# An attention-and-two-MLP kernel: a new hand-written order of the first part, and PSUM pools cut differently

## The chip, the cores and the metric

One core of a Trainium2 chip. The metric is the device time of one execution in microseconds, from the first to the last instruction and what lies around them. TensorE is called PE, VectorE DVE, ScalarE ACT, GpSimd POOL and SyncE SP, as in the profile.

## What is computed

Attention over 4 batches, 8 heads, 576 positions of 64 features: a downsampled attention (mean of four positions, repeated four times) plus a local one within a band of 3 positions. Its output is the input `x` (2304 x 512) of two MLPs, all in float32:

```python
out_d = sm_attn(q_d, k_d, v_d)                      # on means over 4 positions
out_up = np.repeat(out_d, factor, axis=2)
scores = np.where(np.abs(pos[:, None] - pos[None, :]) < factor, scale * q @ k.T, -1e9)
attn_out = out_up + softmax(scores) @ v
h = x @ w_in                                        # 512 -> 2048
x2 = (h * np.cos(h)) @ w_out                        # 2048 -> 512
out = ((x2 @ w_a) * (x2 @ w_b)) @ w_out2            # 512 -> 1536 -> 512
```

## The kernel before

The weights arrive as float64 and are turned into float32 on the chip. Matrix products in float32 are made of three passes with a rounded high part and a low remainder of each operand (`mm3`, L575 to L579, printed as L576, L577 and L578 in the profile), so every operand has to be split: a copy that rounds (the high part, "hi" or "gh") and a subtraction (the low part, "lo" or "gl").

There are two parts. The first runs attention (8 units of 288 rows) and the first MLP (7 blocks of 288 or 432 rows and 16 slices of 128 features, cut to 112 steps), and prepares the weights of the second MLP. The second part is the second MLP, in which each product is made of seven smaller ones (P1 to P7) with sums before and after; its order comes from loops and is not part of the list below.

The first part's order is written out by hand: `ORDER` is a list of 2791 keys, and a loop (L933) takes them one by one and calls the function behind each. `InOrder` (L192) then ties each engine's instructions to the order in which they were written; between the engines only data and free buffers make one wait for the other. A key with `@a`, `@d` or `@p` also says which engine runs it: ACT, DVE or POOL. SP's loads and stores have keys of their own (L, F and S) and go through one queue in the order of the list.

The keys that matter here:

- `w<t>.0` to `w<t>.4`: weight tile t from float64 to float32 and split. 0 and 1 on ACT (L275, L278), 2 on DVE (L280, all operands in SBUF), 3 the rounded copy (L292 on ACT, L294 on DVE), 4 the remainder (L569, DVE or POOL).
- `h<g>.<c>`: the three matmuls of input chunk c of step g into a bank of PSUM ("h", two of them). `c<g>.0` to `c<g>.6`: h times cosine of h. 0 on ACT, 1 on DVE (L629, reads PSUM), 2 on ACT, 3 square (L634 ACT or L636 DVE), 4 on DVE (L638, reads PSUM and frees the h bank), 5 rounded copy gh (L292 or L294), 6 remainder gl (L644, DVE or POOL). `b<g>.<m>`: the matmuls into the four banks "acc".
- attention of unit u: `sm` and `vs` sums over four positions (a reduction on DVE, L360 and L351, or three additions on POOL, L362 to L364, L353 and L355), `lp`, `dp` scores, `lm` and `dx` maxima (L390, L395, L413), `lu`, `da` subtractions, `le`, `de` exponentials, `ln`, `dn` sums, `lz`, `dz` divisions, `lt`, `dt` transposes, `lc`, `dc` copies back, `at` products, `up`, `cb` sums of the two, `xh`, `xl` the split of the result into the tile `xbig` (L294 or L292, and L550).
- `p<n>.*`: weights of the second MLP, converted, combined and stored to DRAM; `x<i>.*`: loads, sums and splits of the second MLP's first input; `F`: its first weight loads.

PSUM has eight banks: four "acc", two "h" and one tile "att" of two banks for attention, all from one pool `ps`. In the second part `banks_of` (L999) hands them out as two sets of four, set 0 being the two halves of "att" and the two "h". `split_g` (L968) also borrows banks of the set that is not in use for a copy of gh (L988), four at a time.

Of the kernel before, what the change touches and what calls it, by code (L numbers as in the profile page):

```python
# [48 lines left out]
L0s2 vs0.2@p h1.1 le0.1 ln0.1 lz0.1@d w2.3@a w2.4@d w4.3@a w4.4@p L0w7 w7.1@a w7.0@a w3.4@p lt0.1 lc0.10@d lc0.11@a L0w5 w5.0@a w5.1@a w7.2@d w5.2@d  # L49
at0.1 up0.1@a cb0.2 xh0.2@d xl0.2@p h0.2 cb0.3 h1.2 L0w6 w6.0@a xh0.3@d xl0.3@p h0.3 w6.1@a w6.2@d w5.3@a w5.4@p Lc8 w8.1@a w8.0@a Lq1.0 sm1.0@d  # L50
w6.3@a Lq1.1 sm1.1@d w8.2@d Lq1.2 h1.3 w6.4@p c0.0@a c1.0@a c0.1@d c0.2@a Lc10 lp1.0 c1.1@d c1.2@a lm1.0 lu1.0@p w8.3@d c0.3@a Lc12 lu1.1@p Lc11
c0.4@d c0.5@d c0.6@p dp1.0 dx1.0 c1.3@a c1.4@d w8.4@p da1.00@d c1.5@d c1.6@p Lq2.2 h2.0 h2.1 h2.2 h2.3 da1.01@d sm1.2@p w12.0@a w10.0@a Lq1.3 sm1.3@d
le1.0 ln1.0 Lk2.2 b0.3 Lk2.3 Lc14 b0.1 h3.0 c2.0@a lz1.0@p h3.1 c2.1@d de1.0 lp1.1 lm1.1 Lc9 b1.1 w11.0@a lu1.3@p b1.3 dn1.0 dz1.1@p b0.2 w11.1@a h3.2
h3.3 w11.2@d c2.2@a Lk2.0 Lq2.1 dp1.1 dx1.1 Lc18 c3.0@a c2.3@a w10.1@a c2.4@d w7.3@a w14.0@a lu1.2@p c3.1@d c3.2@a Lw2.0 b1.2 da1.10@d c2.5@d b0.0 L0V
da1.11@d b1.0 w11.3@d w10.2@d dz1.0@p h4.0 h4.1 h4.2 w9.1@a h4.3 c4.0@a c2.6@p lt1.0 lc1.01@d w7.4@p w9.0@a w9.2@d b2.1 c3.3@a b2.2 b2.3 b2.0 lc1.00@a
c3.4@d Lc13 Lc15 w11.4@p w9.3@d w9.4@p dt1.0 dc1.0@d h5.0 h5.1 w10.3@d w10.4@p Lk2.1 le1.1 ln1.1 lz1.1@p w12.1@a c4.1@d c3.5@d h5.2 h5.3 w14.1@a de1.1
at1.0 up1.0@a cb1.0 Lq2.0 cb1.1 c3.6@p w12.2@d lt1.1 b3.2 w13.1@a c4.2@a xh1.0@d lc1.10@a dn1.1 w14.2@d c4.3@a c4.4@d vs2.0@p c5.0@a b3.1 c5.1@d Lc17
w15.1@a dz1.3@p c4.5@d Lc16 xh1.1@a c5.2@a w12.3@d dz1.2@p xl1.1@d lc1.11@a c4.6@p b3.3 c5.3@a b3.0 c5.4@d w15.0@a h6.0 h6.1 h6.2 w12.4@p h6.3 dt1.1
c6.0@a sm2.0@d c5.5@d h7.0 dc1.1@a h7.1 h7.2 c6.1@d w15.2@d w14.3@a w13.0@a w13.2@d w16.0@a at1.1 up1.1@a cb1.2 w16.1@a b4.2 cb1.3 w16.2@d c6.2@a
xl1.0@p Lc27 w14.4@p Lw2.1 vs2.1@p Lc19 h7.3 c7.0@a c7.1@d b4.1 c6.3@a c6.4@d xh1.2@a xl1.2@p xh1.3@a xl1.3@p c7.2@a sm2.1@d b4.0 Lc21 w13.3@a c5.6@p  # L60
w19.1@a Lc25 lp2.0 b4.3 c7.3@a lm2.0 c7.4@d h8.0 h8.1 h8.2 w17.1@a h8.3 c8.0@a c8.1@d dp2.0 Lw2.2 w13.4@p c6.5@a c6.6@d Lq2.3 h9.0 vs2.2@p h9.1 h9.2
dx2.0 Lc20 w21.0@a b5.2 lu2.0@p da2.01@d h9.3 b5.1 Lq3.0 Lc28 da2.00@d w17.0@a b5.0 b6.0 sm2.2@d lu2.1@p lp2.1 c8.2@a w15.3@a c7.5@a w15.4@p c7.6@p
c8.3@a c8.4@d c9.0@a c9.1@d b5.3 h10.0 h10.1 w19.0@a w19.2@d lm2.1 le2.0 b6.2 ln2.0 Lw2.3 vs2.3@p c9.2@a h10.2 h10.3 lu2.2@p c10.0@a c10.1@d c9.3@a
c9.4@d Lv2 b6.1 b7.1 e7.1@a lu2.3@p b7.0 e7.0@d c8.5@a c8.6@p c10.2@a c10.3@a Lq3.2 Lc26 sm2.3@d c10.4@d b7.2 b6.3 b7.3 e7.3@d c10.5@d Lw2.4 h12.0
# [1159 lines left out]
```

## Time and profile before

| | us |
|---|---|
| median of 3 runs | 953.74 (951.58 to 954.83) |
| profiled execution | 953.3 |
| its span, first to last instruction | 951.4 |
| PE busy | 898.7 |
| DVE busy | 729.0 |
| ACT busy | 574.3 |
| POOL busy | 551.9 |

The profile is of one execution. An engine counts as busy from the start of an instruction to its end, whatever happens in between, so a duration is to be held against the shortest of its kind. The granted clock is TensorE's, as a share of its full speed.

### The profile page before, as it was taken

How to read it: one execution, taken by the hardware profiler on the slowest of the kernel's cores; microseconds unless marked ns; L12 is line 12 of the kernel's file. 1: busy time of each engine (PE TensorE's matmuls, PEld its weight loads, DVE VectorE, ACT ScalarE, POOL GpSimd, SP SyncE). 2: the span in 40 equal slices, each digit the busy share in tenths (PEclk: the TensorE clock that was granted, in tenths of full speed). 3: DMA queues.
4: the chain of work that ended last, by engine and by line, in shares of the span. 5: the costliest groups of instructions: out<-in, count | busy, mean ns of one | idle time of the engine just before them, and what ended most of it. 6: DMA issues, size and time to landing. Idle time of an engine off the chain costs nothing.

```text
span 951.4 us, 18829 instructions
## 1 busy us (share of the span) xinstructions
PE 898.7 (94%) x6828; PEld 862.7 (91%) x6828; DVE 729.0 (77%) x1329; ACT 574.3 (60%) x1237; POOL 551.9 (58%) x689
## 2 busy tenths in 40 slices
PE   3688979999999999999989999999999999999998
PEld 2587878999999999899989899999999999999997
DVE  6999998888698986864688488869667678767754
ACT  5797867565486785843675355548544466544473
POOL 5697879365266773721473266746467754677540
PEclk9789999999999999999999999999999999999999
DMA  9475622245465676400798145594753266832631
GB/s 294 166 264 192 189 83 67 64 129 158 122 207 172 183 203 187 139 21 7 241 308 251 60 151 165 173 401 168 243 211 111 89 245 238 317 109 71 220 148 51
DMA packets 97582, 162.13 MB, mean 170 GB/s; under 512 B 6736, under 2 KB 63568, under 8 KB 97488
## 3 DMA queue, kind: packets, MB, share of 16 engines
q1 hardware_dynamic: 97488, 160.92, 51.0%
q8 instruction: 54, 0.88, 0.4%
q14 instruction: 40, 0.33, 0.1%
HBM read 127.66 MB, written 33.23 MB: 169 GB/s over the span
## 4 chain that ended last, share of the span: by engine, by line
PE 73%; DVE 15%; issue 5%; POOL 3%; ACT 3%; DMA 1%; SPq 0%; DVEq 0%; POOLq 0%; ACTq 0%
PE z L576 14%; PE z L578 13%; PE z L577 13%; PE h L576 5%; PE h L577 5%; PE h L578 5%; PE acc L576 5%; PE acc L577 4%; PE acc L578 4%; DVE raw L280 2%; DVE gs L638 1%; DVE gs L629 1%; PE att L510 1%; PE att L383 1%; PE att L503 1%
## 5 line engine op out<-in xcount | busy, mean ns | idle before, releaser
L966 POOL TENSOR_TENSOR sb<-w,sb 128x256 fp32r<-128x256 f32 x154 | 124.7, 821 | 112.8 <-ACT sb L964 104.8
L576 PE MATMUL h<-xbig,w 128*128 128x288 f32 (+1 forms) x448 | 147.3, 329 | 14.8 <-DVE gs L638 12.3
L576 PE MATMUL acc<-gh,w 128*128 128x288 f32 (+1 forms) x448 | 144.1, 322 | 0.8 <-DVE yp L613 0.8
L577 PE MATMUL h<-xbig,w 128*128 128x288 f32 (+1 forms) x448 | 142.0, 317 | 1.5 <-DVE xbig L550 1.2
L578 PE MATMUL h<-xbig,w 128*128 128x288 f32 (+1 forms) x448 | 141.9, 317 | 0.0
L577 PE MATMUL acc<-gl,w 128*128 128x288 f32 (+1 forms) x448 | 140.8, 314 | 1.0 <-POOL gl L644 0.6
L578 PE MATMUL acc<-gh,w 128*128 128x288 f32 (+1 forms) x448 | 140.2, 313 | 0.0
L964 ACT ACTIVATE sb<-w 128x256 fp32r<-128x256 f32 x252 | 97.6, 414 | 64.2 <-PE z L578 54.9
L644 POOL TENSOR_TENSOR gl<-gs,gh 128x288 fp32r<-128x288 f32 (+1 forms) x66 | 64.9, 986 | 91.0 <-DVE gh L294 59.3
L576 PEld LDWEIGHTS h<-xbig,w 128*128 128x128 f32 x448 | 86.0, 192 | 21.6 <-DVE gs L638 15.8
L576 PE MATMUL z<-xbig,sb 128*128 128x384 f32 x288 | 97.6, 341 | 2.7 <-DVE g L1027 1.3
L578 PE MATMUL z<-xbig,sb 128*128 128x384 f32 x288 | 97.0, 338 | 0.2 <-POOL sb L966 0.2
L577 PE MATMUL z<-xbig,sb 128*128 128x384 f32 x288 | 97.1, 337 | 0.0
L627 ACT ACTIVATE gs<-h 128x288 int32<-128x288 f32 (+1 forms) x112 | 49.3, 440 | 68.3 <-PE h L578 63.8
L577 PEld LDWEIGHTS h<-xbig,w 128*128 128x128 f32 x448 | 86.2, 192 | 2.9 <-DVE xbig L550 1.4
L576 PEld LDWEIGHTS acc<-gh,w 128*128 128x128 f32 x448 | 84.7, 189 | 4.4 <-issue 2.2
L577 PEld LDWEIGHTS acc<-gl,w 128*128 128x128 f32 x448 | 84.7, 189 | 2.8 <-POOL gl L644 1.1
L578 PEld LDWEIGHTS h<-xbig,w 128*128 128x128 f32 x448 | 86.1, 192 | 1.0
L578 PEld LDWEIGHTS acc<-gh,w 128*128 128x128 f32 x448 | 84.5, 189 | 1.0
L631 ACT ACTIVATE gs<-gs 128x288 f32<-128x288 f32 (+1 forms) x112 | 53.4, 477 | 46.8 <-DVE gs L629 46.3
L966 DVE TENSOR_TENSOR sb<-w,sb 128x256 fp32r<-128x256 f32 x98 | 60.6, 621 | 21.1 <-ACT sb L964 20.8
L629 DVE SCALAR_TENSOR_TENSOR gs<-gs,h 128x288 f32<-128x288 int32 (+1 forms) x112 | 54.6, 488 | 27.4 <-ACT gs L627 26.3
(158 smaller groups left out, 2510.2 us busy)
## 6 DMA issues: line engine op xcount, KB each, us to landing
w<-wd SPq DMA_DIRECT2D x63, 512.0 KB
w<-wd_a SPq DMA_DIRECT2D x18, 512.0 KB
w<-wd_b SPq DMA_DIRECT2D x18, 512.0 KB
raw<-in_w_in_dram SPq DMA_DIRECT2D x16, 512.0 KB
raw<-in_w_out_dram SPq DMA_DIRECT2D x16, 512.0 KB
w<-wd_a SPq DMA_DIRECT2D x18, 384.0 KB
w<-wd_b SPq DMA_DIRECT2D x18, 384.0 KB
praw<-in_w_a_dram SPq DMA_DIRECT2D x12, 512.0 KB
```

The costliest lines, as they stand in the source:

```text
L280: dve.scalar_tensor_tensor(out=lw if out is None else out, in0=hh, scalar=3, in1=lw, op0=ALU.logical_shift_left, op1=ALU.bitwise_or)
L383: pe.matmul(p[i][o, W * w:W * w + W], qt[u, 2 * pr + i][r, off:off + W], kt[u // 2, 2 * pr + i][r, BASE[half] + off:BASE[half] + off + W], ...
L503: pe.matmul(p[i][64 * a:64 * a + 64, NB:NB + QD], vdt[b, hp][:, a, c], pd[u, hp][:, 2 * a + c], start=(c == 0), stop=(c == 1),)
L576: i = pe.matmul(ps_out, lh, rh, start=start, stop=False, skip_group_check=more)
L577: pe.matmul(ps_out, lh, rl, start=False, stop=False, skip_group_check=more)
L578: pe.matmul(ps_out, ll, rh, start=False, stop=stop, skip_group_check=more)
L627: act.activation(out=gs[g].bitcast(I32), in_=hps[g], func=AF.Copy, scale=1.0 / (2.0 * math.pi))
L629: dve.scalar_tensor_tensor(out=gs[g], in0=gs[g].bitcast(I32), scalar=-2.0 * math.pi, in1=hps[g], op0=ALU.mult, op1=ALU.add)
L631: act.activation(out=gs[g], in_=gs[g], func=AF.Sin, scale=0.5)
L644: eng.tensor_tensor(out=gl[g], in0=gs.pop(g), in1=gh[g].bitcast(F32), op=ALU.subtract)
L964: act.activation(out=t[:, 0], in_=blk, func=AF.Copy)
L966: (dve if nst[0] % (C["SD"] if G else C["SD0"]) == 0 else pool).tensor_tensor(out=t[:, 1], in0=blk, in1=t[:, 0].bitcast(F32), op=ALU.subtract)
```

## The change

The list `ORDER` is replaced. It has the same 2791 keys in another order, and some keys name another engine. The new list was made by a planner that lets an operation of VectorE which works in SBUF alone and an operation of POOL never run at the same time. Of the engines named in the whole list, above all these differ: `w.4` on DVE 2 before and 12 after (on POOL 30 and 20), `c.5` on DVE 65 and 46 (on ACT 47 and 66), `c.3` on DVE 41 and 36, `c.6` on DVE 46 and 51, `vs` on DVE 10 and 12, `xl` on DVE 9 and 12, `lz` on DVE 2 and 4.

Beside it, attention's tile "att" moves to a pool `pa` of its own, which closes with attention's SBUF pool. The second part opens a pool `pz` in its place with two tiles of one bank each, and the borrowed banks for L988 are taken one at a time, in turn. The diff, with nearly all lines of the two lists left out:

```diff
 ORDER = """
-L0k0 L0q1 L0q0 sm0.0@d L0k1 L0w1 w1.1@a w1.0@a lp0.0 sm0.1@d lm0.0 dp0.0 dx0.0 da0.01@d da0.00@a L0k2 de0.0 L0s1 L0q2 w1.2@d vs0.1@d lu0.0@p lu0.1@p
-le0.0 sm0.2@p dn0.0 dz0.1@a dz0.0@a dt0.0 L0q3 ln0.0 L0w0 w0.1@a w0.0@a L0k3 lz0.0@p sm0.3@d dp0.1 dx0.1 lt0.0 w1.3@a w1.4@p dc0.0@a da0.11@a da0.10@d
-L0s0 vs0.0@p L0w3 lc0.01@d w0.2@d w0.3@d lc0.00@a de0.1 dn0.1 dz0.3@p L0v w3.0@a at0.0 w3.1@a w3.2@d dz0.2@a up0.0@a cb0.0 cb0.1 L0w4 w0.4@p w3.3@a
-xh0.1@a xl0.1@p xh0.0@d lp0.1 dt0.1 L0w2 w2.1@a w2.0@a xl0.0@d h0.0 h0.1 h1.0 lm0.1 lu0.2@d w2.2@d w4.0@a lu0.3@p w4.1@a w4.2@d L0s3 vs0.3@p dc0.1@a
...
-b109.2 b110.2 b111.2 S111.1 e111.2@a S111.2
+L0k0 L0q0 sm0.0@d L0k1 L0q1 lp0.0 lm0.0 lu0.0@d L0w1 w1.0@a w1.1@a sm0.1@p dp0.0 dx0.0 da0.01@d w1.2@d L0q2 L0k2 sm0.2@d lu0.1@p le0.0 ln0.0 L0s0
+vs0.0@p da0.00@a L0w0 de0.0 lz0.0@d lt0.0 w0.0@a w1.3@a dn0.0 w1.4@d w0.1@a dz0.0@a dz0.1@a dt0.0 w0.2@d w0.3@d L0s1 L0q3 L0k3 sm0.3@d dp0.1 dx0.1
+da0.10@d vs0.1@p L0w2 lc0.00@a L0v w0.4@d lc0.01@a dc0.0@a at0.0 w2.1@a L0s2 w2.0@a w2.2@d w2.3@d w2.4@p da0.11@a de0.1 dn0.1 up0.0@a cb0.0 xh0.0@a
+cb0.1 xh0.1@d dz0.3@a Lq1.0 sm1.0@d lp0.1 lm0.1 lu0.3@d lu0.2@d dz0.2@a xl0.0@p L0w4 h0.0 w4.0@a w4.1@a w4.2@d Lq1.1 sm1.1@d le0.1 w4.3@a L0w3 w3.0@a
...
+b111.0 e111.0@d S111.0
...
@@ -225,6 +225,7 @@
     dram = ctx.enter_context(tc.tile_pool(name="dram", bufs=1, space=bass.MemoryType.DRAM))
     at_ctx = ExitStack()
     at = at_ctx.enter_context(tc.tile_pool(name="at", bufs=1))
+    pa = at_ctx.enter_context(tc.tile_pool(name="pa", bufs=1, space=bass.MemoryType.PSUM))
 
     ident = const.tile([128, 128], F32, name="ident")
     mask = const.tile([128, W], F32, name="mask")
@@ -251,7 +252,7 @@
     def att_ps(u, what, pr):
         tags = first[what, pr] if u == 0 else ("att",)
         if len(tags) == 1:
-            t = ps.tile([128, 2, 512], F32, tag="att", name="att", bufs=1)
+            t = pa.tile([128, 2, 512], F32, tag="att", name="att", bufs=1)
             return t[:, 0], t[:, 1], t
         a, b = (ps.tile([128, 512], F32, tag=t, name="att", bufs=2 if t == "h" else 1) for t in tags)
         return a, b, None
@@ -937,6 +938,7 @@
                 order.settle()
                 at_ctx.close()
                 p2 = ctx.enter_context(tc.tile_pool(name="p2", bufs=1))
+                pz = ctx.enter_context(tc.tile_pool(name="pz", bufs=1, space=bass.MemoryType.PSUM))
                 order = InOrder(tc, (act, dve, pool))
             if e:
                 args.insert(0, eng[e])
@@ -982,9 +984,9 @@
             act.activation(out=gh[k], in_=t, func=AF.Copy)
             hi = gh[k].bitcast(F32)
             if p % 2 and r < NP * len(AB) - 3:
-                if not spare:
-                    spare.extend(banks_of(seg[0] % 2))
-                hi = spare.pop(0)
+                tag, n = BANKS[seg[0] % 2][nst[1] % 4]
+                nst[1] += 1
+                hi = bank(tag, n, "hq")
                 act.copy(out=hi, in_=gh[k].bitcast(F32))
             dve.tensor_tensor(out=gl[k], in0=t, in1=hi, op=ALU.subtract)
             if what == "P2":
@@ -994,20 +996,15 @@
         zlast = [None]
         seg = [0]
 
-        spare = []
-
-        def banks_of(s):
-            if s:
-                return [ps.tile([128, N2], F32, tag=f"acc{m}", name="z") for m in range(4)]
-            a = ps.tile([128, 2, 512], F32, tag="att", name="z", bufs=1)
-            h = [ps.tile([128, N2], F32, tag="h", name="z", bufs=2) for i in range(2)]
-            return [a[:, 0, :N2], h[0], a[:, 1, :N2], h[1]]
+        BANKS = ((("att", 2), ("h", 2)) * 2, tuple((f"acc{m}", 1) for m in range(4)))
+
+        def bank(tag, n, name):
+            return (pz if tag == "att" else ps).tile([128, N2], F32, tag=tag, name=name, bufs=n)
 
         def banks():
             s = seg[0] % 2
             seg[0] += 1
-            spare.clear()
-            return banks_of(s)
+            return [bank(tag, n, "z") for tag, n in BANKS[s]]
 
         def gtile(nm, p):
             if nm in ("B12", "B22"):
```

## Rows read from the trace of the kernel before

**Rows 1.** Busy time by stretch: length, PE, PEld, DVE, ACT, POOL (instructions), clock, DMA, GB/s.
```profile
0.00:25.00 25.00, 9.27 (x129) 7.24 (x129) 16.50 (x31) 14.09 (x42) 13.23 (x26) 1.00 0.93 299
25.00:175.00 150.00, 126.61 (x1340) 116.76 (x1341) 136.52 (x238) 118.57 (x241) 122.26 (x133) 0.93 0.46 152
175.00:500.00 325.00, 320.24 (x2898) 305.25 (x2897) 250.89 (x489) 202.28 (x395) 168.63 (x261) 1.00 0.52 156
500.00:951.40 451.40, 442.58 (x2469) 433.49 (x2467) 325.12 (x574) 239.31 (x561) 247.80 (x270) 1.00 0.51 180
```

**Rows 2.** Chain of waits, 25 to 165 us: shares by line, then pieces (start, us).
```profile
by line: DVE raw L280 11.6%; issue 5.3%; DVE gs L629 4.2%; DVE xbig L550 4.1%; DVE gs L638 4.1%; PE h L577 3.5%; PE h L576 3.4%; DVE xbig L294 3.3%; DVE w L294 3.0%; PE h L578 3.0%; DVE gh L294 2.8%; DVE sl L443 2.6%; POOL vd L355 2.6%; DVE
...
72.89 4.24 DVE xbig L550
119.82 3.19 POOL vd L355
```

**Rows 3.** DVE's instructions by line and form, 25 to 175 us: count, busy us, mean ns.
```profile
L280 DVE SCALAR_TENSOR_TENSOR raw<-raw 128x512 uint32<-128x512 uint32 x29 | 29.6, 1036 | 0.0
L629 DVE SCALAR_TENSOR_TENSOR gs<-gs,h 128x288 f32<-128x288 int32 x29 | 12.8, 440 | 2.8 <-ACT gs L627 2.7
...
L294 DVE CAST gh<-gs 128x288 fp32r<-128x288 f32 x16 | 7.9, 496 | 0.3
L294 DVE CAST w<-raw 128x512 fp32r<-128x512 f32 x9 | 7.1, 793 | 0.1
L550 DVE TENSOR_TENSOR xbig<-xf,xbig 128x288 fp32r<-128x288 f32 x3 | 6.3, 2112 | 0.1
L395 DVE TENSOR_REDUCE mx<-smx 128x10 f32<-128x640 f32 x7 | 5.7, 821 | 0.2
L294 DVE CAST xbig<-xf 128x288 fp32r<-128x288 f32 x6 | 5.7, 956 | 0.1
```

**Rows 4.** Durations by line, whole run: count, shortest/median/longest ns, first and last start.
```profile
L280 DVE SCALAR_TENSOR_TENSOR raw<-raw x32: 658/681/3248, 10.9 to 159.6; 128x512 uint32<-128x512 uint32 x32
...
L294 DVE CAST gh<-gs x65: 295/385/1226, 47.1 to 528.5; 128x288 fp32r<-128x288 f32 x48, 128x432 fp32r<-128x432 f32 x17
L294 DVE CAST xbig<-xf x20: 226/310/2289, 25.1 to 444.4; 128x288 fp32r<-128x288 f32 x14, 128x144 fp32r<-128x144 f32 x6
L294 DVE CAST w<-raw x10: 412/623/1514, 20.0 to 165.0; 128x512 fp32r<-128x512 f32 x10
...
L550 DVE TENSOR_TENSOR xbig<-xf,xbig x11: 299/459/4319, 25.4 to 374.4; 128x288 fp32r<-128x288 f32 x7, 128x144 fp32r<-128x144 f32 x4
...
L569 POOL TENSOR_TENSOR w<-raw,w x30: 1282/1314/2081, 17.3 to 156.3; 128x512 fp32r<-128x512 f32 x30
L569 DVE TENSOR_TENSOR w<-raw,w x2: 809/1010/1211, 33.6 to 166.2; 128x512 fp32r<-128x512 f32 x2
...
L351 DVE TENSOR_REDUCE vd<-vs x10: 1012/1076/1928, 11.8 to 343.8; 72x128 f32<-72x512 f32 x9, 72x256 f32<-72x1024 f32 x1
...
L355 POOL TENSOR_TENSOR vd<-vd,vs x36: 452/464/3184, 19.4 to 340.1; 72x128 f32<-72x128 f32 x30, 72x256 f32<-72x256 f32 x6
```

**Rows 5.** Timeline, DVE at 72.80 us, POOL from 73.51 us: start us, duration us.
```profile
72.80 4.32 DVE L550 TENSOR_TENSOR xbig<-xf,xbig 128x288 fp32r<-128x288 f32 x1
...
73.51 1.28 POOL L569 TENSOR_TENSOR w<-raw,w 128x512 fp32r<-128x512 f32 x1
74.76 0.79 POOL L550 TENSOR_TENSOR xbig<-xf,xbig 128x288 fp32r<-128x288 f32 x1
75.52 1.29 POOL L569 TENSOR_TENSOR w<-raw,w 128x512 fp32r<-128x512 f32 x1
```

**Rows 6.** PE's matmuls by line, 475 to 500 us, with the idle time before them.
```profile
L576 PE MATMUL h<-xbig,w 128*128 128x432 f32 x20 | 7.2, 362 | 2.8 <-DVE gs L638 2.8
```

**Rows 7.** L988: ACT's waits (us, times); busy time over three stretches of 20 us.
```profile
  DVE g L1027: 10.0, 2
...
sum 60.00, PE 60.00 PEld 59.53 DVE 41.51 ACT 31.87 POOL 27.74; mean PE 20.00 PEld 19.84 DVE 13.84 ACT 10.62 POOL 9.25
```

More of the change, by code (lines that the diff above doesn't have):

```diff
@@ L49 @@
[L49 to L64, printed above, removed]
@@ L161 @@
-c96.6@p e95.3@d e95.2@a c99.4@d h100.3 e95.0@a p31.0 h101.0 h101.1 h101.2 h101.3 S95.3 p27.3 p27.4 c99.5@a p28.11 p28.10 p28.12 c100.0@a c100.1@d
-c100.2@a c99.6@d c100.3@d c100.4@d b96.0 S95.2 b96.1 b97.1 S95.0 b96.3 p31.10 b97.3 c101.0@a c101.1@d p29.2 p31.11 p26.0 p31.12 b96.2 b97.2 p32.0
-c101.2@a c100.5@d c100.6@d b97.0 c101.3@a b98.0 c101.4@d h103.0 h103.1 h103.2 h103.3 c101.5@d b98.2 p26.10 p28.2 p28.3 p27.5 p30.0 p28.4 p28.5 p31.2
-p32.10 p32.11 x5.1 p26.11 p32.12 p32.2 c103.0@a c103.1@d b98.3 p26.12 p26.2 c101.6@d c103.2@a c103.3@a c103.4@d b98.1 p31.3 x5.0 p31.4 h102.0 h102.1
@@ L169 @@
-x10.3 p30.5 b101.3 h107.2 h107.3 h108.0 h108.1 h108.2 c104.5@a c106.6@p x10.2 x12.4 h108.3 c107.0@a x10.0 x12.0 c107.1@d c107.2@a c107.3@d c104.6@p
-c108.0@a c108.1@d x12.2 c108.2@a b102.2 b102.3 b102.0 b103.3 c108.3@a b103.2 b102.1 c108.4@d p32.3 b103.1 c108.5@d c108.6@d h109.0 b103.0 c105.5@d
-c107.4@d p32.4 x12.5 h109.1 h109.2 h109.3 c105.6@d h110.0 h110.1 h110.2 h110.3 c109.0@a c109.1@d c109.2@a c109.3@a b104.1 b105.1 b104.3 c109.4@d
-b104.0 h111.0 c110.0@a c110.1@d c110.2@a c110.3@d h111.1 c110.4@d x13.0 p26.5 b104.2 F14 b105.3 b105.2 c110.5@d c110.6@d b105.0 c107.5@d x11.2 h111.2
@@ new lines @@
+b18.3 c20.5@a h22.0 h22.1 h22.2 h22.3 c22.0@a c22.1@d b18.1 w17.3@d w17.4@d b19.1 da3.01@a Lq4.3 c21.5@a c21.6@d w23.2@d c22.2@a c22.3@a lu3.1@p h23.0
+h23.1 c22.4@d sm3.2@p w30.3@a h23.2 h23.3 c23.0@a w30.4@d c23.1@d S15.3 c20.6@p b19.3 b20.3 w25.3@a w25.4@p w23.3@a w23.4@p c23.2@a c23.3@a lp3.1
+lm3.1 h24.0 h24.1 h24.2 c23.4@d h24.3 Lq4.0 b18.0 b19.0 b20.0 b21.0 sm3.3@d c24.0@a c24.1@d w28.3@a w28.4@p dp3.1 dx3.1 da3.10@d b20.2 lu3.2@p
+da3.11@d h25.0 c23.5@a h25.1 h25.2 h25.3 lu3.3@p b21.3 c22.5@a c22.6@d c24.2@a b22.3 c24.3@d le3.0 ln3.0 c23.6@p de3 b21.2 c25.0@a b20.1 b21.1 b22.1
@@ new lines @@
+p25.3 p25.4 c95.5@a h99.0 h99.1 h99.2 h99.3 c95.6@d b94.3 p27.11 c99.0@a b93.2 b93.0 p27.10 b94.1 b95.1 c98.4@d c99.1@d c99.2@a c99.3@a h100.0 p29.0
+p29.11 p29.10 p27.12 b94.2 b95.2 p27.2 c97.5@d c97.6@d b94.0 c99.4@d p25.5 p28.0 p29.12 c98.5@d b95.3 e95.3@d e95.1@a p27.3 p32.0 e95.2@d p27.4 h100.1
+h100.2 h100.3 p28.11 b95.0 S95.3 c98.6@p h101.0 h101.1 h101.2 p28.10 p28.12 h101.3 b96.2 b97.2 e95.0@d b96.0 b97.0 c100.0@a c100.1@d p28.2 c101.0@a
+c101.1@d c101.2@a c101.3@d c101.4@d b96.3 b97.3 p32.10 b96.1 S95.2 p26.0 p26.11 c99.5@a c100.2@a c99.6@d p26.10 h103.0 h103.1 c100.3@d c100.4@d
@@ new lines @@
+c100.5@d h103.2 h103.3 c103.0@a c103.1@d c103.2@a c100.6@d c103.3@d S95.1 h102.0 h102.1 p31.0 p27.5 b97.1 b98.2 S95.0 h102.2 b98.3 b98.1 b99.1 b99.2
+b100.2 p28.3 p28.4 p31.11 c103.4@d p31.10 p29.2 b99.3 p31.12 h102.3 c103.5@a p30.0 p30.10 b98.0 b99.0 p26.12 p30.11 p30.12 c102.0@a c102.1@d x5.1 x8.1
+p28.5 c101.5@a c101.6@d b100.3 h105.0 h105.1 c102.2@a c102.3@a c102.4@d c102.5@a b100.0 b101.0 p31.2 x7.1 h104.0 x9.3 F12 x9.5 h105.2 h105.3 c102.6@d
+b100.1 x5.0 c103.6@d h104.1 h104.2 h104.3 p32.11 b102.0 p32.12 b101.1 p31.3 b101.2 c105.0@a c105.1@d c105.2@a F13 x8.3 c105.3@a c105.4@d c104.0@a
@@ new lines @@
+c104.1@d p30.2 x11.1 x9.1 x10.3 b101.3 c104.2@a c104.3@d x8.0 p26.2 h106.0 h106.1 h106.2 h106.3 p30.3 c105.5@a c104.4@d b102.2 p29.3 p30.4 p30.5
+c104.5@a p29.4 p29.5 b102.1 c106.0@a c104.6@p c106.1@d c106.2@a b102.3 c106.3@a c106.4@d h108.0 b103.2 h108.1 h108.2 h108.3 c108.0@a x12.1 b103.1 x7.0
+c108.1@d x8.2 x11.0 b103.3 c106.5@d c106.6@p b103.0 x9.0 b104.0 c105.6@p F14 h107.0 h107.1 h107.2 h107.3 c108.2@a c108.3@a c108.4@d c108.5@a x9.2
+h109.0 h109.1 h109.2 p31.4 p31.5 c107.0@a c107.1@d x12.5 h109.3 b104.2 p26.3 x10.0 p26.4 b104.3 c107.2@a c107.3@a c107.4@d c109.0@a c109.1@d c109.2@a
@@ new lines @@
+c109.3@a c109.4@d x10.2 b104.1 c107.5@d p32.2 p32.3 h110.0 b105.0 h110.1 c107.6@d h110.2 h110.3 c108.6@p b105.2 c110.0@a c110.1@d c110.2@a b105.1
+p26.5 x9.4 F15 x10.1 p32.4 h111.0 h111.1 h111.2 x12.3 c110.3@a c110.4@d x12.0 x12.2 h111.3 b105.3 p32.5 c111.0@a x13.0 x12.4 c111.1@d c111.2@a x13.1
+x11.3 c111.3@a c111.4@d b106.2 b107.2 b106.0 b106.1 b107.0 b106.3 b107.3 b107.1 c110.5@d b108.1 c109.5@d c109.6@d c110.6@d c111.5@a c111.6@d b108.3
+b109.1 b110.1 b111.1 e111.1@d S111.1 b109.3 b110.3 b111.3 e111.3@d b108.2 b109.2 b110.2 b111.2 S111.3 e111.2@d S111.2 b108.0 x11.2 b109.0 b110.0
```

208 lines of the change are left out of this document (106 added, 102 removed).

## The prediction, before the result was known

> **What bounds the kernel now.** I read the stages first [rows 1]. TensorE (PE) is busy for 442.58 of the last 451.4 us and 320.24 of the 325 us before them, so after 175 us there are some 14 us to win in all, the last store included. The first 175 us hold 39: 15.7 idle in the first 25, and 23.4 in the 150 that follow, where VectorE (DVE) is the busy one with 136.52 of 150. TensorE's clock is 0.93 of full there, as against 1.00 later, so the true loss is somewhat larger. The chain of waits for 25 to 165 us [rows 2] says the same: before the row is cut off it names eight groups of DVE with 35.7% of the stretch, and among its longest pieces are single instructions that took far too long, 4.24 us of DVE and 3.19 us of POOL. So the first part is bound at its start by DVE, later by PE, and the second part by PE.
>
> **How much of DVE's busy time is work.** The groups of DVE between 25 and 175 us [rows 3] stand beside the shortest or median time of the same instruction [rows 4]. Instructions that read PSUM take there what they always take (L629 440 ns). So do reductions that read SBUF alone (L395 821 ns). The others that work in SBUF alone are stretched: L280 29.6 us for 29, which at 658 ns are 19.1, so 10.5 over; casts to gh 7.9 against 16 x 0.295, 3.2 over; casts to w 7.1 against 9 x 0.412, 3.4; L550 6.3 against 3 x 0.459, 4.9; casts to xbig 5.7 against 6 x 0.310, 3.8. That is 25.8 us in which DVE stands with an instruction started (smaller groups left out). The timeline shows on what [rows 5]: an L550 that needs 0.46 us began at 72.80 and took 4.32, until the third of three POOL instructions in a row was over. POOL suffers in turn: the 3.19 us on the chain [rows 2] are one L355, whose median is 0.46 [rows 4]. So the two engines do exclude each other, and whoever has its next instruction ready tends to keep going.
>
> **The new order.** All 2791 keys remain; their places and some engines change. I counted the keys ahead of h24.0, by which 31 of 32 w.4 tasks are listed now (the last ends near 167 us, [rows 4]). POOL's instructions there fall from 127 to 99: 11 fewer w.4 (1.282 us each, 14.1), 4 fewer vs (three of 0.45 each, 5.4), 4 fewer c.6 (0.79, as the L550 of the same size in [rows 5], 3.2), the rest about 4 by the same kind of count; 27 us less. DVE gets 8 of these w.4 (0.81, the shortest seen, so 6.5 us; the other 3 come behind h24.0), 4 vs (L351, 1.076, 4.3) and 3 c.6 (0.459, as L550, 1.4) [rows 4]; what else moves nets about -1.5, above all 5 casts to gh that go to ACT. **DVE gets 10.7 us more work** ahead of the same matmuls, ACT about none. What DVE's extra instructions delay are the L629 and L638 queued behind them, and PE waits on L638 for its next h bank.
>
> **What that costs.** If all of DVE's work lay on the chain the price would be 10.7; if only the named 36%, 3.8. I take 6, since DVE is 91% busy but the chain also runs over PE, ACT and POOL.
>
> **What it gives back.** The stalls of 25.8 us. Lower end: nothing synchronizes the two engines, only each engine's own order is fixed; stalls then go by POOL's count (99/127) times that of DVE instructions that can be stretched (87 against 76), which is 0.89, and 2.8 us come back. Upper end: stalls go with the cases where such a DVE instruction stands directly behind a POOL key among these two engines' keys. These fall from 25 to 12, while those behind another of DVE's own kind rise from 16 to 35. That is 0.48, and 13.4 come back. I take 10, nearer to the upper end, because of the train in [rows 5]: two of its three are w.4, of which POOL loses over a third, and shorter trains shorten stalls by more than in proportion. I count the stalls in full on the chain, as its longest pieces are such stalls [rows 2]. POOL's own waits on the chain (3.19 us for vd) shrink as well: -1 (0 to -2).
>
> At this place the Trainium skill has a rule ("SBUF — State Buffer", section "Who interferes with whom"): whichever of the two engines starts first holds the shared pair of ports for that instruction, the other blocks until it finishes, and on trn2 a reduction never contends. The second half agrees with L395 [rows 3], and speaks against a plan that keeps reductions and POOL apart. The first half would let an instruction stall for one POOL instruction at most; [rows 5] shows three.
>
> **Loads and the end of the first part.** SP's loads are reordered with the rest. The four ahead of the first scores are the same, and 4.49 MB stand ahead of at0.0 in both orders, so the start costs 0 (if a load were late, 1 to 2 us, since DMA is 93% busy in the first 25 us [rows 1]). The conversions p29 to p32 and the sums and splits x are spread anew where PE now has its one long gap of the later first part, 2.8 us on L638 [rows 6]: -1, between -2.8 and +2.8. The last splits of x move behind h111.0, but 72 matmuls are listed behind it, so they are covered.
>
> **The PSUM pools.** Attention's two-bank tile gets its own pool, and the second part's banks 0 and 1 become two tiles of one bank; spare copies (L988) take one bank at a time instead of four. What can go are waits of ACT such as two on L1027, 10.0 us together [rows 7]. PE was busy for 60.00 of 60 us around these and a third, so I count 0. With the cover gone they would cost their 5 us each; at best it returns 1 us of PE's 8.8 idle in the last stretch.
>
> **Sum.** -10 + 6 - 1 - 1 = -6. The profiled execution took 953.3 us (span 951.4), the median is 953.74; so 947.3, said as **947.5**. With all ends together: -13.4 + 3.8 - 2 - 2.8 - 1 = -15.4, and -2.8 + 10.7 + 2.8 + 2 = +12.7. All at one end is unlikely; for 8 in 10 I take 938 to 960.
>
> **The rivals.**
> Slower: DVE stays the bound with more work. The moved vs and w.4 queue ahead of L629 and L638, and POOL's trains form again as POOL starts when its inputs are there. Stalls fall by 2.8, work of 10.7 comes: +7.9, so 961.2; with half of the added work hidden, 955.9. It decides as soon as less than about 11 us of stall disappear and all the added work is on the path. For it: DVE is busy for 136.52 of 150 us [rows 1], and reductions given to DVE (vs) buy nothing at the port. Against it: the chain names POOL and ACT pieces as well, and POOL loses a fifth of its load. I take 958. Chance 0.25. The skill's rule (the same section) leads here: with stalls of one POOL instruction at most they fall in proportion only.
> No change: the order across the engines is not enforced, so the exclusion that the plan was made with is only partly met; 6 to 10 us of stall go, as much work comes. 953.5. Chance 0.23. For it: the two terms are about as large.
> The PSUM pools are what counts: 1 us of PE's idle time, more only if PE's clock or a bank wait that I don't see depends on it; 952.3 with the rest zero. That falls into no change as well, and the 0.23 includes it.
>
> **How the numbers follow.** My forecast has 0.52, slower 0.25, no change 0.23. About 0.3% (2.9 us) is what a measurement of this kernel can tell from no change. The forecast's own range is 938 to 950.5; with the slower rival up to 960 and no change within, some 2 in 10 are left outside.
>
> **What would show it.** Right: between 25 and 175 us L280 falls from 1036 ns towards 800, POOL's busy time from 122 to about 95, DVE's busy time stays near 135 with more instructions in it, and PE's gains some 5 us; after 175 us PE is as now, with the gap before 500 us at or under 2.8. Wrong: L280 still near 1000 ns and PE's waits on L638 longer in that stretch (slower), or PE idle for more than 5 us between 175 and 475, which would mean that DVE has no slack left there (slower); gains that appear after 500 us would mean the pools.

## The result, and the profile after

The changed kernel takes **929.14 us** (median; 925.76 to 930.92) against 954.29 us for the kernel before, run beside it on the same chip: a ratio of 0.9737, with a 95% interval of 0.9703 to 0.9772. The forecast was 947.5 us, with a range from 938 to 960. The sign was right and the size was not: 25 us went where 6 were expected, and the time lies below the range. The profiled execution took 928.92 us with a span of 927.1.

The stages of the profile after, with the columns of [rows 1] (length, then PE, PEld, DVE, ACT and POOL with instructions, clock, DMA share, GB/s):

```profile
0.00:25.00 25.00, 11.00 (x165) 8.37 (x165) 16.66 (x37) 14.63 (x46) 12.94 (x27) 1.00 0.93 270
25.00:175.00 150.00, 134.28 (x1426) 125.63 (x1425) 137.91 (x265) 122.61 (x254) 93.24 (x108) 0.92 0.49 163
175.00:500.00 325.00, 323.80 (x2850) 309.39 (x2849) 232.48 (x467) 204.67 (x403) 157.66 (x250) 1.00 0.52 159
500.00:927.10 427.10, 422.66 (x2394) 421.01 (x2392) 318.17 (x565) 234.32 (x551) 245.35 (x271) 1.00 0.52 185
```

Between 25 and 175 us PE is busy for 7.7 us longer than in [rows 1], DVE as long as before but with 265 instructions in place of 238, and POOL for 29 us less. The clock plays no part: 0.92 against 0.93 there, 1.00 in both later.

DVE's groups in that stretch, as in [rows 3] (the changed file's lines are one higher: L280 is L281, L294 is L295, L629 is L630, L550 is L551):

```profile
L281 DVE SCALAR_TENSOR_TENSOR raw<-raw 128x512 uint32<-128x512 uint32 x29 | 24.9, 866 | 0.5 <-ACT raw L279 0.4
L630 DVE SCALAR_TENSOR_TENSOR gs<-gs,h 128x288 f32<-128x288 int32 x32 | 14.1, 444 | 3.5 <-ACT gs L628 3.4
...
L396 DVE TENSOR_REDUCE mx<-smx 128x10 f32<-128x640 f32 x7 | 5.7, 820 | 0.2
...
L295 DVE CAST w<-raw 128x512 fp32r<-128x512 f32 x10 | 5.0, 497 | 0.1
...
L295 DVE CAST gh<-gs 128x288 fp32r<-128x288 f32 x12 | 4.4, 376 | 0.6 <-DVE gs L639 0.5
...
L551 DVE TENSOR_TENSOR xbig<-xf,xbig 128x288 fp32r<-128x288 f32 x5 | 3.1, 660 | 0.0
...
L295 DVE CAST xbig<-xf 128x288 fp32r<-128x288 f32 x5 | 2.3, 453 | 0.1
```

What reads PSUM (L630) and what reduces (L396) takes the same time as before. What works in SBUF alone has come down: L281 from 1036 to 866 ns, casts to w from 793 to 497, to gh from 496 to 376, to xbig from 956 to 453, L551 from 2112 to 660. I added up, for all of DVE's SBUF-only instructions that start between 25 and 175 us, without the reductions, the reciprocals and tensor_scalar, by how much each exceeds a short duration of its shape (the 15th percentile in the trace of before). This **stretch** was 29.9 us in 81 instructions and is 15.3 us in 93.

Where the time went is seen best by one matmul's start. The first matmul of h24 moved from 154.5 to 144.5 us, that of h64 from 312.5 to 298.2, and the second part's first (tile z) from 540.6 to 525.6. So 15.0 us are won in the first part. From its first z matmul to its last, the second part took 407.0 us and takes 397.7: another **9.3 us**, where I had counted none. The two windows around one place of it (same columns) and the waits there:

```profile
850.00:900.00 50.00, 49.03 (x277) 48.20 (x277) 36.24 (x64) 22.30 (x56) 32.89 (x40) 1.00 0.36 125
```

```profile
840.00:890.00 50.00, 50.00 (x287) 50.00 (x286) 34.73 (x64) 24.64 (x60) 32.53 (x38) 1.00 0.52 190
```

The first is of before, the second of after: in the same 50 us PE gets through 287 matmuls in place of 277. Ten matmuls fewer at 175 ns are 1.75 us, yet the window of before shows an idle time of 0.97. The timeline of before tells why (start, duration, engine, what ended the idle time):

```profile
857.07 0.34 PE L576 MATMUL z<-xbig,sb 128*128 128x384 f32 x1
...
857.41 0.55 DVE L1027 TENSOR_TENSOR g<-g,z 128x384 f32<-128x384 f32 x1
...
858.01 0.44 PE L576 MATMUL z<-xbig,sb 128*128 128x384 f32 x1 [0.61 <-DVE g L1027]
...
858.29 0.34 PE L577 MATMUL z<-xbig,sb 128*128 128x384 f32 x1
...
858.47 0.34 PE L578 MATMUL z<-xbig,sb 128*128 128x384 f32 x1
```

A matmul is drawn 0.34 us long, but the next starts 0.175 us after it. A start that is up to 0.17 us late therefore shows no idle time at all, and a longer wait shows that much too little. By starts, 49 of the 2268 z matmuls of before come over 20 ns late, together 9.1 us; in after none does. The DVE instruction at 857.41 reads the result of the product P3 for one factor, in one half of the two-bank tile; the matmul that waits for it begins P3 for the other factor, in the other half. PE's waits in the second part of before, from the view of waits (us, times, longest), name the partner:

```profile
PE z L576 <- DVE g L1027: 1.9, 4, 0.6
PE z L576 <- DVE ev L1027: 1.3, 1, 1.3
```

Both rows are missing in after.

### The profile page after: what moved, and what is told of

Read it like the earlier page. It is cut to its first block, busy times and chain, and to the rows that moved or that the text cites. A ratio compares the mean times of both kernels' runs of the same rounds, so it can differ in the third digit from the quotient of the medians.

```text
span 927.1 us, 18811 instructions
## 1 busy us (share of the span) xinstructions
PE 891.7 (96%) x6828; PEld 864.4 (93%) x6828; DVE 705.2 (76%) x1332; ACT 576.2 (62%) x1249; POOL 509.2 (55%) x654
## 4 chain that ended last, share of the span: by engine, by line
PE 81%; DVE 10%; ACT 3%; issue 3%; POOL 2%; DMA 0%; SPq 0%; POOLq 0%; DVEq 0%; ACTq 0%
PE z L578 14%; PE z L577 14%; PE z L579 14%; PE acc L577 6%; PE h L577 6%; PE acc L578 6%; PE acc L579 6%; PE h L579 5%; PE h L578 5%; DVE raw L281 1%; PE att L384 1%; DVE gs L639 1%; PE att L511 1%; PE att L476 1%; PE att L504 1%
## 5 line engine op out<-in xcount | busy, mean ns | idle before, releaser
L577 PEld LDWEIGHTS h<-xbig,w 128*128 128x128 f32 x448 | 86.2, 192 | 14.2 <-DVE gs L639 11.2
L645 POOL TENSOR_TENSOR gl<-gs,gh 128x288 fp32r<-128x288 f32 (+1 forms) x61 | 59.4, 980 | 69.9 <-ACT gh L293 35.0
L630 DVE SCALAR_TENSOR_TENSOR gs<-gs,h 128x288 f32<-128x288 int32 (+1 forms) x112 | 54.9, 491 | 37.0 <-ACT gs L628 36.7
```

What stands on the lines that cost most here:

```text
L577: i = pe.matmul(ps_out, lh, rh, start=start, stop=False, skip_group_check=more)
L630: dve.scalar_tensor_tensor(out=gs[g], in0=gs[g].bitcast(I32), scalar=-2.0 * math.pi, in1=hps[g], op0=ALU.mult, op1=ALU.add)
L645: eng.tensor_tensor(out=gl[g], in0=gs.pop(g), in1=gh[g].bitcast(F32), op=ALU.subtract)
```

## The experiments

**The order alone, and the pools alone.** The first kernel has the new list and the old PSUM tiles; its edit undoes the new pools in the changed kernel:

```diff
-            t = pa.tile([128, 2, 512], F32, tag="att", name="att", bufs=1)
+            t = ps.tile([128, 2, 512], F32, tag="att", name="att", bufs=1)
...
-                tag, n = BANKS[seg[0] % 2][nst[1] % 4]
-                nst[1] += 1
-                hi = bank(tag, n, "hq")
+                if not spare:
+                    spare.extend(banks_of(seg[0] % 2))
+                hi = spare.pop(0)
...
+            a = ps.tile([128, 2, 512], F32, tag="att", name="z", bufs=1)
+            h = [ps.tile([128, N2], F32, tag="h", name="z", bufs=2) for i in range(2)]
+            return [a[:, 0, :N2], h[0], a[:, 1, :N2], h[1]]
```

> The new list with the PSUM pools of before. Theory A (two separate gains): the first matmul of the second part starts near 525.6 us as after the change (540.6 before), and the second part keeps the length of before, 407.0 us from its first to its last matmul start; about 939 us. Theory B (the second part runs better because the first hands over differently): the second part takes about 398 us as after the change, and the time is about 929 us.

It took 938.48 us, a ratio of 0.9851 (0.9829 to 0.9874). The first z matmul started at 527.4 us, nearly where after has it, and the second part took 406.7 us, as before. Its waits of PE from 530 us on are those of before:

```profile
PE z L576 <- DVE g L1027: 2.2, 5, 0.6
PE z L576 <- DVE ev L1027: 2.0, 2, 1.3
```

The second kernel has the old list, in place of the new one, in the changed kernel:

```diff
-L0k0 L0q0 sm0.0@d L0k1 L0q1 lp0.0 lm0.0 lu0.0@d L0w1 ...
+L0k0 L0q1 L0q0 sm0.0@d L0k1 L0w1 w1.1@a w1.0@a lp0.0 sm0.1@d ...
```

> The list of before with the new PSUM pools. Theory A: first part as before (540.6 us), second part 398 us, with none of PE's waits on DVE; about 945 us. Theory B: no change, about 953 us. The prediction on record counted these pools at 0 to 1 us.

It took 943.77 us, 0.9911 (0.9882 to 0.994). The first z matmul started at 538.8 us and the second part took 398.4. So the two parts of the change are nearly independent, and the runs put a price on each: against after, the order is worth 14.6 us (943.77 - 929.14) and the pools 9.3 (938.48 - 929.14), together 24.0 of the 25.2. The ratios to before give 16.6 and 10.9 us instead, so each price is good to some 2 us. Both traces with the new pools also reach h24 some 1.8 us earlier than the trace with the same list and the old ones (152.6 against 154.5, 144.5 against 146.2), so a little of the 15.0 us of the first part may belong to the pools; these are single executions.

**What it is in the pools.** Two things changed there: banks 0 and 1 of the second part became two tiles of one bank, and spare copies take one bank at a time. Each was put back alone; in the first of these kernels the spare copies of set 0 come from the two "h" banks only, as "att" is a pair again.

```diff
-        BANKS = ((("att", 2), ("h", 2)) * 2, tuple((f"acc{m}", 1) for m in range(4)))
+        BANKS = ((("h", 2),) * 4, tuple((f"acc{m}", 1) for m in range(4)))
...
-            return [bank(tag, n, "z") for tag, n in BANKS[s]]
+            if s:
+                return [bank(tag, n, "z") for tag, n in BANKS[s]]
+            a = pz.tile([128, 2, 512], F32, tag="att", name="z", bufs=1)
+            h = [bank("h", 2, "z") for i in range(2)]
+            return [a[:, 0, :N2], h[0], a[:, 1, :N2], h[1]]
```

> The changed kernel, but the second part's two z banks of set 0 are again the halves of one two-bank tile; the spare copies are taken one bank at a time (in set 0 from the two h banks alone). Theory E (a matmul into one half waits for DVE's reads of the other half, because both are one tile): the second part takes about 407 us again instead of 398, with PE waiting on DVE L1027; about 938 us in all. Theory F (it was the spare copies, taken four banks at a time): about 929 us.

With the two-bank tile back, the time is 938.0 us (0.9828; 0.9784 to 0.9871) and the second part takes 406.2. PE's waits return:

```profile
PE z L577 <- DVE ev L1028: 2.0, 2, 1.3
PE z L577 <- DVE g L1028: 1.9, 4, 0.6
```

By starts, these six matmuls come 0.5 to 1.5 us late. Counted along the second part they are the same six that wait for L1027 in before, and, with a seventh, with the order alone.

```diff
-                tag, n = BANKS[seg[0] % 2][nst[1] % 4]
-                nst[1] += 1
-                hi = bank(tag, n, "hq")
+                if not spare:
+                    spare.extend(bank(tag, n, "hq") for tag, n in BANKS[seg[0] % 2])
+                hi = spare.pop(0)
...
```

> The changed kernel, but spare banks for the copies of gh are taken four at a time and dropped at the next set, as before; z keeps its one-bank tiles. Theory E: the second part keeps its 398 us, about 929 us. Theory F: about 407 us and 938 us, with waits of ACT of 5 to 8 us at the starts of the three back phases.

With the spare banks taken four at a time the time is 929.65 us (0.9751; 0.9715 to 0.9787), that of after. Nearly the whole gain of the pools comes from the first, 8.4 us between these two kernels: a matmul into one half of a two-bank tile waits for DVE's read of the other half, as the order between them is kept by tile. ACT's waits of 10.0 us on L988 [rows 7], from which the prediction judged the pools, had nothing to do with it: in after ACT's copy still waits 14.7 us in three waits on DVE, and PE loses nothing.

```profile
ACT hq L990 <- DVE g L1024: 14.7, 3, 5.0
```

**Engines without places, and places without engines.** Can the order's gain be put down to one of the two? One kernel has the old places with the engines of the new list, one the new places with the old engines, both with the new pools. The edit is the list alone; how its first line begins in the one, against the old list, and in the other, against the new:

```diff
-L0k0 L0q1 L0q0 sm0.0@d L0k1 L0w1 w1.1@a w1.0@a lp0.0 sm0.1@d ...
+L0k0 L0q1 L0q0 sm0.0@d L0k1 L0w1 w1.1@a w1.0@a lp0.0 sm0.1@p ...
...
-L0k0 L0q0 sm0.0@d L0k1 L0q1 lp0.0 lm0.0 lu0.0@d ...
+L0k0 L0q0 sm0.0@d L0k1 L0q1 lp0.0 lm0.0 lu0.0@p ...
```

> The keys stand in the order of before, but each runs on the engine that the new list names; new PSUM pools. Theory C (it is POOL's smaller load that frees DVE): the second part starts near 530 us, more than half of the 15 us gained; about 934 us. Theory D (it is the places, which keep the two engines apart): it starts at 538 us or later, since DVE has more work and nothing is kept apart; about 943 us or more.

> The keys stand in the new order, but each runs on the engine of the list of before; new PSUM pools. Theory C: little of the 15 us is left, the second part starts at 537 us or later; about 942 us. Theory D: most is left, it starts at 530 us or earlier; about 934 us.

They took 993.54 us (1.044; 1.0402 to 1.0479) and 991.23 us (1.0412; 1.0377 to 1.0446), some 50 us beyond the times that were expected (934 to 943). The windows of the first (columns as in [rows 1]) show that no engine is as busy in its first part as DVE is in both real kernels:

```profile
25.00:175.00 150.00, 118.89 (x1214) 107.70 (x1215) 120.24 (x226) 111.05 (x227) 85.41 (x90) 0.94 0.46 152
175.00:500.00 325.00, 302.73 (x2779) 285.40 (x2778) 218.76 (x452) 182.63 (x368) 141.88 (x230) 0.96 0.40 117
```

PE is idle for 22 us in a stretch (175 to 500 us) where both real kernels idle for under 5. My reading is that each engine's queue is run in order, and that a task that is moved to another engine at its old place stands there ahead of tasks whose inputs come earlier; the waits of these two kernels were not taken apart, so this is not shown. Stretch falls in both (14.2 us in 84 instructions, 16.7 in 71), but with every engine waiting more that says nothing about the exclusion. So this pair tells only that places and engines fit each other.

**Single groups of tasks given back to POOL.** In the changed kernel's list, eleven w.4 go back, or eight vs.

```diff
-... w7.4@d ...   (eleven such)
+... w7.4@p ...
```

> The changed kernel with eleven w.4 tasks back on POOL, where the list of before had them, at their new places. Theory G (long POOL trains are what stalls DVE): DVE's stretched instructions lose 22 us or more instead of 15 between 25 and 175 us, and the time rises by 5 us or more, to 934 or above, although DVE has some 7 us less work. Theory H (the prices of the prediction: 0.21 us of stall for each us of POOL, 14.1 x 0.21 = 3.0, against 6.5 x 0.56 = 3.6 us of DVE work saved): within 3 us of the changed kernel.

934.26 us (0.98; 0.9764 to 0.9836), so 5.1 us more than after: the time that theory G forecast, but not by its cause. Stretch rose only from 15.3 to 17.3 us, less than the 22 that the theory asked. A wait of nearly 5 us stands in another row. PE's waits from 25 to 175 us, and POOL's timeline before the longest of them:

```profile
PE h L577 <- DVE gs L639: 4.5, 5, 1.7
PE acc L578 <- POOL gl L645: 4.4, 1, 4.4
```

```profile
139.64 1.62 POOL L570 TENSOR_TENSOR w<-raw,w 128x512 fp32r<-128x512 f32 x1 [1.57 <-DVE w L295]
141.23 1.17 POOL L401 TENSOR_TENSOR smx<-smx,mx 128x320 f32<-128x320 f32 x1
142.36 0.31 POOL L363 TENSOR_TENSOR qd<-q 128x72 f32<-128x72 f32 x1
...
143.52 1.29 POOL L570 TENSOR_TENSOR w<-raw,w 128x512 fp32r<-128x512 f32 x1
144.77 0.80 POOL L645 TENSOR_TENSOR gl<-gs,gh 128x288 fp32r<-128x288 f32 x1
```

One matmul waits 4.4 us for a gl that starts at 144.77, behind six POOL instructions in a row, two of them w.4. In after the gl at this place in the order starts at 140.01. So w.4 on POOL cost by POOL's own queue, not only through the port. DVE is busy for some 5 us less here between 25 and 175 us, and the first matmul of h24 still starts 3.2 us later than in after (147.7).

```diff
-... L0s3 vs0.3@d ...   (eight such)
+... L0s3 vs0.3@p ...
```

> The changed kernel with eight vs sums back on POOL, as in the list of before, at their new places: 24 POOL instructions more, 8 reductions of 1.07 us less on DVE. Theory G: slower by 3 us or more, since trains of three more POOL instructions stall DVE. Theory H, and the prediction's remark that reductions given to DVE buy nothing at the port: no slower than the changed kernel, 927 to 930 us.

928.56 us (0.9753; 0.9702 to 0.9805), the same as after, as expected: reductions given to DVE buy nothing. Stretch between 25 and 175 us is 20.1 us here, 4.8 more, and DVE has 6.2 us of reductions less to do there (five of the eight).

**The port by itself.** This kernel leaves all of the reference's work out and runs ten DVE instructions of one kind, first alone and then beside eight POOL subtractions of 128x512:

```python
for f in (two, cast, red, psum, scal, mixed):
    for k in (0, 8):
        act.activation(out=g, in_=d, func=AF.Identity, bias=q[:, :1])
        if k:
            train(k)
        f(10)
```

> Only ten DVE instructions of one kind at a time on 128x512 float32, first alone and then beside eight POOL subtractions on SBUF; the rest of the computation is left out. Theory L (two-input work and casts within SBUF exclude POOL, reductions and reads of PSUM don't): subtractions and casts take some 0.68 and 0.41 us alone and several times that, up to the whole POOL train of 8 x 1.3 us, in single instructions beside POOL; reductions and PSUM reads take the same in both. Theory M (everything within SBUF excludes POOL, as the planner had it): reductions stretch as well. By the Trainium skill (SBUF — State Buffer, Who interferes with whom) one instruction waits for one POOL instruction at most, so no single one should exceed about 2 us.

The timeline of DVE, each pair alone and then beside POOL (start, us for all ten), and under it POOL's eight (beside two-input DVE work, casts, reductions, and at 124.92 alone):

```profile
3.30 7.23 DVE L63 TENSOR_TENSOR d<-g,s 128x512 f32<-128x512 f32 x10 [1.36 <-ACT g L92]
11.38 14.76 DVE L63 TENSOR_TENSOR d<-g,s 128x512 f32<-128x512 f32 x10 [0.85 <-ACT g L92]
27.01 4.58 DVE L67 CAST e<-g 128x512 fp32r<-128x512 f32 x10 [0.87 <-ACT g L92]
...
32.64 12.10 DVE L67 CAST e<-g 128x512 fp32r<-128x512 f32 x10 [0.85 <-ACT g L92]
...
45.82 7.17 DVE L71 TENSOR_REDUCE m<-g 128x8 f32<-128x512 f32 x10 [0.87 <-ACT g L92]
...
54.04 7.17 DVE L71 TENSOR_REDUCE m<-g 128x8 f32<-128x512 f32 x10 [0.85 <-ACT g L92]
```

```profile
11.49 13.37 POOL L88 TENSOR_TENSOR q<-g,s 128x512 f32<-128x512 f32 x8 [10.24 <-ACT g L92]
32.75 11.24 POOL L88 TENSOR_TENSOR q<-g,s 128x512 f32<-128x512 f32 x8 [7.89 <-ACT g L92]
54.15 10.65 POOL L88 TENSOR_TENSOR q<-g,s 128x512 f32<-128x512 f32 x8 [10.16 <-ACT g L92]
...
124.92 10.64 POOL L88 TENSOR_TENSOR q<-g,s 128x512 f32<-128x512 f32 x8 [0.83 <-ACT g L100]
```

Subtractions and casts lose 7.5 us to POOL's train of 10.6; reductions lose nothing and cost POOL nothing; DVE subtractions that read PSUM took 7.22 us both times, and tensor_scalar behaved as the cast (4.58 and 12.10). The longest single subtraction took 1.63 us against 0.69 alone: 0.94 more, less than one POOL instruction (1.26 alone). So theory L divides the instructions rightly, but no single one waited for a whole train. Where PSUM readers and SBUF ones took turns, the SBUF ones rose only from 0.69 to between 0.91 and 1.19 us.

**POOL's load at a fixed list.** Two kernels cut POOL's w.4 from 512 to 128 columns (the low parts of the other columns are left out, and the third matmul of each three reads the first 128 instead), one in the old list with the new pools, one in the new list. A third carries out each of POOL's w.4 twice.

```diff
-            eng.tensor_tensor(out=t[:, 1], in0=raw[:, :, 0].bitcast(F32), in1=t[:, 0].bitcast(F32), op=ALU.subtract)
+            q = slice(0, 128) if eng is pool else slice(0, 512)
+            eng.tensor_tensor(out=t[:, 1, q], in0=raw[:, q, 0].bitcast(F32), in1=t[:, 0, q].bitcast(F32), op=ALU.subtract)
...
```

> The list of before with the new PSUM pools (943.8 us without this), with POOL's 30 w.4 subtractions cut from 512 to 128 columns; the low parts of those weights are left out for the other columns, and the first MLP's third pass reads the first 128. POOL loses about 25 us of work. Theory J (DVE's stalls behind POOL set the first part's time): stalls between 25 and 175 us fall from 29 to 20 us or less and the time falls by 7 us or more, to 937 or less. Theory K (DVE's own work and the order set it): within 3 us of 943.8.

> The changed kernel (929.1 us without this) with POOL's 20 w.4 subtractions cut in the same way; POOL loses about 17 us. Theory J: fewer stalls are left to win, the time falls by 2 to 5 us. Theory K: within 2 us of 929.1.

```diff
+            for rep in range(2 if eng is pool else 1):
                 eng.tensor_tensor(out=t[:, 1], ...
```

> The kernel after, in which each of POOL's twenty w.4 is carried out twice in a row (the second writes the same values into the same place), so POOL gets 20 x 1.28 = 25.7 us more and its busy time between 25 and 175 us should come near the 122 us that it had before, while the order of the list stays the new one. Theory P (the halved stalls come from POOL's lower load, as old_list_short_w4 has 13.9 us at a busy time of 100.6): the time by which DVE's SBUF-only instructions there exceed their shortest goes from 15.3 us back to 25 to 30. Theory Q (they come from the places in the new list): it stays at or under 20 us. For the total, with the 0.47 us per us of POOL that old_list_short_w4 and pools_only differ by, 12 us more: 941 us, 935 to 947 by either theory; if POOL's load counts by its own queue alone, as the one wait of 4.4 us on POOL's gl in w4_on_pool says, 934 to 940.

They took 932.01 us (0.9774; 0.9744 to 0.9803), 921.34 us (0.9658; 0.9627 to 0.9689) and 940.95 us (0.9874; 0.9825 to 0.9923). The old list gains 11.8 us, as POOL is busy for 25.6 us less in the whole run, the new one gains 7.8 for 18.1 less (more than the 2 to 5 expected), and it loses 11.8 for 29.1 more, each time against the kernel with the same list and pools: between **0.4 and 0.5 us for each us of w.4 on POOL**. This is a price for w.4 that is taken away or added with nothing in return. With eleven w.4 given back POOL is busy for 13.4 us more and the kernel takes 5.1 us longer; with the vs sums it is 12.3 us more and no time. For the kernel with w.4 twice, PE's waits between 25 and 175 us show where some of the loss is:

```profile
PE acc L579 <- POOL gl L646: 3.9, 2, 2.4
...
PE acc L580 <- POOL w L571: 3.1, 2, 2.2
```

In after neither row is there.

Stretch between 25 and 175 us in the kernels that keep places and engines together:

| kernel | list | POOL busy, us | DVE's SBUF-only instructions | stretch, us | per instruction, us |
|---|---|---|---|---|---|
| before | old | 122.3 | 81 | 29.9 | 0.37 |
| pools alone | old | 122.9 | 82 | 29.2 | 0.36 |
| old list, short w.4 | old | 100.6 | 87 | 13.9 | 0.16 |
| new list, w.4 twice | new | 118.0 | 84 | 22.2 | 0.26 |
| w.4 on POOL | new | 102.5 | 81 | 17.3 | 0.21 |
| vs on POOL | new | 102.3 | 93 | 20.1 | 0.22 |
| after | new | 93.2 | 93 | 15.3 | 0.16 |
| new list, short w.4 | new | 80.4 | 98 | 8.3 | 0.08 |

The kernel with w.4 twice was to decide between load (25 to 30 us of stretch) and places (at most 20). It gave 22.2, so neither: with nearly the old load, 6.9 of the 14.6 us come back. And the old list with a lighter POOL has no more stretch than the new one. POOL's load moves the stretch in both lists, and the places may hold a part of it, but no kernel here separates them; the repeated w.4 may also be a milder load than others, as the last section shows. For the time the same question is open: the eleven w.4 on DVE are worth 5.1 us of the order's 14.6 and the eight vs nothing, and what the other moved tasks and the places share of the remaining 9 to 10 us no run tells.

## Why the prediction was wrong, step by step

**What bounds the kernel.** Right for the first part: DVE is still busy for 137.91 of 150 us. For the second part the reading failed. "At best it returns 1 us of PE's 8.8 idle" took PE's busy time for its progress; by the starts of matmuls 9.1 us were late there, of which 4.4 showed as idle time before them.

**The PSUM pools: 0, measured 9.3.** This is the step whose mechanism was wrong. The prediction followed the one wait that it connected with the edit, ACT's on L1027 [rows 7], and found PE fully busy around it. That was true and beside the point. The rows to read were PE's own waits on L1027 in the second part, shown above: they are small (3.2 us as idle time), but they name the partner, and the partner reads a bank of the tile whose other half PE is about to write. The prediction itself said that gains after 500 us would mean the pools, and so it was. With the order's gain, forecast as 6 and measured as 14.6, this put the time outside the range; either error alone would have left it just inside (938.48 us was measured for the order alone, and 947.5 - 9.3 is 938.2).

**Stalls: -10, measured about -16.** The mechanism was right and its size too small. Up to the start of h24, stretch fell from about 30 to 14 us, by more than the upper end of 13.4, and the time in which DVE does nothing from 18.3 of 154.54 us to 15.7 of 144.45. How much of the 16 us reached the total is not shown by itself. The upper end counted places in a list that nothing enforces across engines. The runs speak for POOL's load, but with a steeper law than the 0.89 of the lower end: 18% less POOL in the old list (122.9 to 100.6 us) took away 52% of the stretch. The sentence that "shorter trains shorten stalls by more than in proportion" is what they bear out.

**More work for DVE: +6; the work was about +10, its price is open.** Up to h24 DVE's instructions, at short durations, sum to some 117 us in before and 127 in after, about 10 more, near the 10.7 that were counted. That DVE stands idle for 15.7 of the 144.45 us there speaks for much of it being on the way to h24. The kernel with eleven w.4 back on POOL speaks against a price of its own: DVE has less to do there, and h24 starts 3.2 us later. Up to h24 the gain was 10 us, from 154.5 to 144.5, where stalls and work together were forecast at 4. The stretch alone fell by 6 us more than forecast; what the added work cost is not shown.

**POOL's own waits: -1.** About right in the rows that it named: PE's waits on vd (2.2 us in before) are gone in after, and those on smx fell from 2.5 to 1.9. PE's waits on L639, which would have grown if the added work had queued ahead of it, fell from 9.4 us (L638 in before) to 6.1. But the two kernels with more w.4 on POOL show what the term left out: PE waits 4.4 us (once) and 3.9 us (in two waits) for gl on POOL there, 0.5 in before. What DVE does in POOL's place shortens POOL's queue, and the prediction priced that queue at 1 us.

**The loads and the end of the first part: -1.** The gap before 500 us [rows 6] shrank: PE is idle for 1.2 us there in place of 2.8. The start was not zero, the first matmul of h0 going from 27.4 to 25.0 us, but at h4 0.8 of this is left. From h24 to the first z matmul another 4.9 us were won (386.05 us became 381.18), where the sum had 1: PE is busy for 378.9 and 378.5 us there, and its idle time fell from 7.1 to 2.7. Which waits these were was not taken apart.

**The rule on the ports.** "SBUF — State Buffer", section "Who interferes with whom", of the Trainium skill says that reductions never contend on trn2. The kernel of the port agrees (7.17 us both times), and so does the kernel with vs on POOL in its time. That rule was the best hint against the change's giving vs to DVE, and it came out as no gain and no loss. Its other half is that whichever engine is first keeps the ports for its whole instruction. Read as a wait of one instruction at most, it agrees with the port kernel (0.94 us at the longest) and not with [rows 5] or a row below.

**The rivals.** The slower one needed two things: that the added work lies on the path and that less than 11 us of stall disappear. The second did not come true, as some 16 went; whether the first did is not shown. No change rested on the two terms being alike; the added work was 10 and the stall that went 16. The pools as "what counts" was the rival nearest to the surprise, and its price was bounded at 1 us by a row that can't show it. Of the signs: L280 fell to 866 ns (towards 800), POOL to 93.2 us (about 95), DVE stayed at 137.9 with 27 more instructions, PE gained 7.7 (some 5). They came true, and still the sum was short. The one sign for the later stages, that PE after 175 us would be as now, failed: PE's idle time between 175 and 500 us fell from 4.8 to 1.2 us, and the second part is 9.3 us shorter.

## What to carry to other kernels

Where matmuls are drawn longer than the distance at which they start, count a late start by the starts, and not by PE's idle time: the second part here showed 4.4 us before its matmuls and lost 9.1. Two banks that different engines use at different times should be two tiles, because the order between their users was kept by tile here; look for PE's short waits on the engine that reads the other half. Giving POOL's SBUF work to DVE is judged by who waits for it in POOL's queue, and by the stretch: here w.4, for which PE waits, brought 5.1 us for 13.4 us of POOL, and vs brought nothing for 12.3. Engines and places of this list could not be changed one without the other.
